# The last 28 static columns of each expert: 1188 instead of 1216 in an attention and mixture-of-experts kernel

## The chip, the core and the metric

The kernel runs on one core of a Trainium2 chip. The metric is the device time of one execution in microseconds (us), the median of several runs. Engines are named as the profile names them: PE is TensorE's matmul, PEld its weight load, DVE is VectorE, ACT is ScalarE, POOL is GpSimd, SP is SyncE, which here only issues DMAs.

## The reference

Attention over 8 batches, 8 heads, 576 rows and 64 columns is followed by a mixture of 8 experts over the 4608 rows that attention gives. Each row goes to the two experts with the largest noisy logits:

```python
noisy_logits = x @ w_gate + np.log1p(np.exp(x @ w_noise)) * noise
top2 = np.argpartition(-noisy_logits, 2, axis=1)[:, :2]
for e in range(E):
    for k in range(2):
        mask = top2[:, k] == e
        h = np.maximum(x[mask] @ w1[e], 0.0)             # 512 -> 1024
        out[mask] += top2_w[mask, k, None] * (h @ w2[e])  # 1024 -> 512
```

How many rows an expert gets depends on the data. All inputs are drawn by `setup_inputs` from seed 0.

## The kernel before, in words

**Attention** (the first 600 us or so) runs in steps of a pair of heads, with loads, splits, scores and stores placed by hand at slots of a schedule. As each batch ends, its rows are routed: for each row and choice a slot number `e * slots + rank` is worked out, and the pair (row number, gate weight) is written with an indirect DMA into a table in DRAM, `slot_table` (L614). An expert owns `slots` consecutive entries of it. The first `cap = 32 * NBLK` of them (L30: NBLK is 38, so 1216) are the static part, which the unrolled program always computes. Entries that no row fills point at spare rows with a gate of zero; the initial contents are written early by SP (`table_part`, L466 to L471). Rows beyond `cap` go to `overflow` (L1084), a loop behind the static program that takes 128 rows in each pass and makes as many passes as the counts ask for.

**Experts.** The static part of an expert is cut into 38 blocks of 32 entries, in three groups of 12, 12 and 14 blocks (L31), that is 384, 384 and 448 columns. In float32r each operand is split into a high and a low part, and a product is three matmuls. For each group:

- `gather` (L846, POOL) fetches up to 128 rows of x with an indirect DMA, `bounce` (L856, SP) stores them to a staging buffer in DRAM, `load` (L866, SP) reads them back with four DMAs in another order, and `turnx` (L878 to L881, DVE and ACT) transposes and splits them.
- `layer1` (L883) makes 8 pieces f of the hidden layer; each is 12 matmuls over all columns of the group, `n = 32 * GROUPS[g]` (L885, L896).
- `layer2` (L902) makes the output. In its usual form a unit holds up to 128 rows as the weights of 24 matmuls with 512 moving columns (L917). For the last 10 blocks of the third group `layer2t` (L952) swaps the operands: four chains c of 24 matmuls whose moving operand has `n = 32 * WIDE[g]` = 320 columns (L956, L966). The last expert has no wide part: its third group is computed by four usual units, the last of them with 64 rows.
- The result is multiplied by the gate (L919, or L971 and L976) and added to `out` by an indirect DMA (L938, POOL).

`run` (L1018) writes these steps out in a fixed order for the 8 experts; while the matmuls of one group run, the next groups are fetched and the weights of the next stage loaded and split. Two PSUM tiles named `sp` of two banks each take the layer2 results.

**Tokens.** `tokens` (L808) copies an expert's table entries into the tile `ti` with four DMAs on SP, one for each quarter of the partitions, and `index` (L819) derives from it on DVE the row numbers for the gathers (`sx`, `ix`) and the gates (`gw`). For the experts from 2 on this is one part of 38 blocks, loaded one expert ahead. Experts 0 and 1 have two parts (`parts_of`, L112): the first 24 (12) blocks hold rows of the first six batches and are read while attention still runs; the rest, 14 (26) blocks, can be read only when the last batch is routed. These eight DMAs, for both experts in a row, are issued at one place (`tokb`, L55), and both `index` calls stand together behind them (`ixb`). This is the handover from attention to the experts: group 2 of expert 0 cannot be gathered before.

**The start.** The constructor of `Experts` (L705) runs before `attention` records anything, so what it puts on POOL stands ahead of `make_identity` (L137), whose result the first ten matmuls (L141) read.

Of the kernel before, what the change touches and what calls it, by code (L numbers as in the profile page):

```python
# [26 lines left out]
SPARE = 384  # L27
NB = 5

NBLK = 38  # L30
GROUPS = (12, 12, 14)  # L31

WIDE = (0, 0, 10)

STAGED = 20

EARLY = (GROUPS[0] + GROUPS[1], GROUPS[0])
WARM = 10

SCHED = dict(  # L40
# [19 lines left out]
@with_exitstack  # L60
def tile_attention_moe(ctx: ExitStack, tc, q, k, v, tau, wgn, noise, noise_r, w1, w2, out, x_dram, table, stage):
    nc = tc.nc
    const = ctx.enter_context(tc.tile_pool(name="const", bufs=1))
    cap = 32 * NBLK
    nover = -(-max(N - cap, 0) // 128)
    slots = cap + 128 * nover
    state = dict(cap=cap, nover=nover, slots=slots)
    with tc.manual_schedule(), ExitStack() as c:
        work = c.enter_context(tc.tile_pool(name="work", bufs=1))
        psum = c.enter_context(tc.tile_pool(name="psum", bufs=1, space=PSUM))  # L70
        experts = Experts(tc, const, work, psum, state, w1, w2, out, x_dram, table, stage)
        attention(tc, const, work, psum, state, q, k, v, tau, wgn, noise, noise_r, out, x_dram, table, experts)
        experts.run(lambda: overflow_count(tc, const, work, state) if nover else None)
    if nover:
        with ExitStack() as c:
            overflow(c, tc, const, state, w1, w2, out, x_dram, table)


def wide(e, g):

    return 0 if e == E - 1 else WIDE[g]


def units(e, g):
# [27 lines left out]
def parts_of(e):  # L112


    n = EARLY[e] if e < len(EARLY) else 0
    return [(0, n), (n, NBLK - n)] if n else [(0, NBLK)]


def attention(tc, const, work, psum, state, q, k, v, tau, wgn, noise, noise_r, out, x_dram, table, experts):
    nc = tc.nc  # L120
    rot = Rotor()
    slots, cap, nover = state["slots"], state["cap"], state["nover"]
# [317 lines left out]
    base = state["base"] = const.tile([128, E], F32, name="base")  # L440
# [3 lines left out]
    def init_parts():  # L444
        def load_noise():
            nc.sync.dma_start(nz[:, :, 0:4, :], noise)
            nc.sync.dma_start(nz[0:64, :, 4, :], noise_r)
        yield load_noise


        nb = 4 * -(-NBLK // 4)
        tin = work.tile([32, nb, 2], I32, name="tin", tag="y1")
        vec.memset(tin, 0)
        for a in range(0, nb, 12):
            m = min(12, nb - a)
            gp.iota(tin[:, a:a + m, 0], pattern=[[32, m]], base=0, channel_multiplier=1)
        tin = tin.rearrange("p a c -> p (a c)")
        if nover:
            tin2 = work.tile([nover, 128, 2], I32, name="tin2", tag="y0")
            vec.memset(tin2, 0)  # L460
            gp.iota(tin2[:, :, 0], pattern=[[1, 128]], base=0, channel_multiplier=0)
            tin2 = tin2.rearrange("p a c -> p (a c)")
        z = work.tile([128, DM], F32, name="zeros", tag="zeros")
        vec.memset(z, 0.0)

        def table_part(e):  # L466
            to = table[e * slots:(e + 1) * slots, :].rearrange("s c -> (s c)")
            for k0, nb in parts_of(e):
                nc.sync.dma_start(to[64 * k0:64 * (k0 + nb)].rearrange("(p c) -> p c", p=32), tin[:, 0:2 * nb])
            if nover:  # L470
                nc.sync.dma_start(to[2 * cap:2 * slots].rearrange("(p c) -> p c", p=nover), tin2)  # L471
        for e in range(E):
            yield lambda e=e: table_part(e)
        yield lambda: nc.sync.dma_start(x_dram[0:SPARE, :].rearrange("(a p) d -> p a d", p=128),
                                        z[:, None, :].to_broadcast([128, SPARE // 128, DM]))
        nt = (N + SPARE) // 128

        def out_part(a):
            m = min(2, nt - a)
            nc.sync.dma_start(out[128 * a:128 * (a + m), :].rearrange("(a p) d -> p a d", p=128),  # L480
                              z[:, None, :].to_broadcast([128, m, DM]))
        for a in range(0, nt, 2):
            yield lambda a=a: out_part(a)
# [157 lines left out]
    for n in range(NP):  # L641
        g = 9 * n
# [29 lines left out]
        if n % HP == HP - 1:  # L672
# [10 lines left out]
            for i in range(2 * NB):  # L683
                to = g + x + 11 + i
                if experts and b >= B - 2:
                    to = G + START["put" if late else "put0"][i]
# [15 lines left out]
class Experts:  # L702


    def __init__(self, tc, const, work, psum, state, w1, w2, out, x_dram, table, stage):  # L705
# [10 lines left out]
        for j in range(4):  # L716
# [2 lines left out]
        self.toks = [tuple(const.tile([128] + sh, t, name=f"{n}{i}") for n, sh, t in  # L719
                           (("ti", [NBLK, 2], I32), ("ix4", [NBLK], I32), ("sx", [nm], I32), ("gw", [nm], F32)))  # L720
                     for i in range(3)]
        self.chunks = [(e, l, f) for e in range(E) for l in range(2) for f in range(8)]
        self.at = {c: i for i, c in enumerate(self.chunks)}
        CW = 32 * max(GROUPS)
# [83 lines left out]
    def tokens(self, e, part):  # L808
        if e >= E:
            return  # L810
        nc = self.nc
        ti, ix, sx, gw = self.tok[e] = self.toks[e % 3]
        k0, nb = parts_of(e)[part]
        src = bass.AP(tensor=self.table.tensor, offset=self.table.offset + (e * self.slots + 32 * k0) * 2,
                      ap=[[2 * nb, 32], [1, 2 * nb]])
        for j in range(4):
            nc.sync.dma_start(ti[32 * j:32 * j + 32, k0:k0 + nb].rearrange("p k c -> p (k c)"), src)

    def index(self, e, part):  # L819
        if e >= E:  # L820
            return
        vec = self.nc.vector
        ti, ix, sx, gw = self.tok[e]
        k0, nb = parts_of(e)[part]
        vec.tensor_scalar(ix[:, k0:k0 + nb], ti[:, k0:k0 + nb, 0], 4.0, self.jq, op0=ALU.mult, op1=ALU.add)
        for j in range(4):
            k = slice(k0 + j, k0 + nb, 4)
            n = len(range(k.start, k.stop, 4))
            p = slice(32 * j, 32 * j + 32)
            vec.tensor_copy(sx[p, k0 // 4:k0 // 4 + n], ti[p, k, 0])  # L830
            vec.tensor_copy(gw[p, k0 // 4:k0 // 4 + n], ti.bitcast(F32)[p, k, 1])
# [50 lines left out]

    def layer1(self, e, g, f):  # L883
        nc = self.nc
        n = 32 * GROUPS[g]  # L885
        if f == 0:
            self.ht[e, g] = (self.next("h", 2), [])
        xh, xl = self.xt[e, g] if f < 7 else self.xt.pop((e, g))
        p, parts = self.ht[e, g]
# [12 lines left out]
    def layer2(self, e, g, i):  # L902
        nc = self.nc
        t = (GROUPS[g] - wide(e, g)) // 4
        if wide(e, g) and i >= t:
            return self.layer2t(e, g, i - t)
        _, parts = self.ht[e, g]
        _, _, sx, gw = self.tok[e]
        m = 32 * min(4, GROUPS[g] - 4 * i)
        t = self.first[g] // 4 + i  # L910
        ps = self.bank(False)
        c = slice(128 * i, 128 * i + m)
        for f in range(8):
# [4 lines left out]
        y = self.place()  # L918
        nc.vector.tensor_scalar(y[0:m].rearrange("p (j c a) -> p c j a", j=4, c=4),  # L919
                                ps[0:m].rearrange("p (c j a) -> p c j a", c=4, j=4), gw[0:m, t:t + 1], None, op0=ALU.mult)  # L920
        self.late.append((self.turn["y"], lambda: self.scatter(
            e, range(4 * t, 4 * t + m // 32), self.out, sx[0:m, t:t + 1], y[0:m])))

    def place(self):

# [8 lines left out]
    def scatter(self, e, blocks, out, idx, y):  # L934
# [3 lines left out]
        st = self.nc.gpsimd.indirect_dma_start(out=out, out_offset=bass.IndirectOffsetOnAxis(ap=idx, axis=0),  # L938
                                               in_=y, in_offset=None, compute_op=ALU.add)

        own = {(k - k0) % 12 for k in blocks for k0, nb in parts_of(e) if k0 <= k < k0 + nb}
        key = tuple(sorted(own))
        self.tc.declare_no_dep(st.ins, group=f"out{e}.{key}", reason="other rows")
        for r in SETS:
# [7 lines left out]
    def layer2t(self, e, g, i):  # L952


        nc = self.nc
        nb, n = WIDE[g], 32 * WIDE[g]  # L956
        k0 = GROUPS[g] - nb
        _, parts = self.ht[e, g]
        ti, ix, _, _ = self.tok[e]
# [233 lines left out]
```

## Time and profile before

| | |
|---|---|
| runs | 1488.08, 1491.34, 1493.65 us, median 1491.34 us |
| profiled execution | 1489.61 us, of which the span from the first to the last instruction is 1487.9 us |
| busy, share of that span | PE 98%, PEld 81%, DVE 60%, ACT 47%, POOL 44% |
| mean granted TensorE clock | 0.990 of full speed |
| DMA | 220.55 MB, 148 GB/s over the span |

The profile is of one execution. A busy PE is one that has a matmul in flight; matmuls are pipelined, so the time that a matmul adds is read from the distance between the starts of successive ones, not from the length of one. A line number is that of the kernel before; in the changed kernel the same lines stand 12 to 25 lines further down (layer1's matmul is L921, layer2t's L991, layer2's L942).

### The profile page before, as it was taken

Reading aid. Unit: us, or ns where it says so; the run is one execution under the profiler, and the core shown is the slowest. Engines: PE = TensorE matmul, PEld = TensorE weight load, DVE = VectorE, ACT = ScalarE, POOL = GpSimd, SP = SyncE. Lnnn points to the kernel's source line nnn. Section 1 sums busy time; section 2 is a strip of 40 time slices with the busy share of each in tenths; the row PEclk is TensorE's granted clock in tenths of the full one; section 3 lists DMA queues with packets and bytes.
Section 4 is the critical chain, followed back from the end, with each engine's and each line's share of the span. In section 5 each row is a group of like instructions: output and inputs, shape, how many; then the busy total and the mean of one; then the engine's idle time right before and its main releaser. Section 6 shows DMA issues by size and latency. Waiting matters only on the chain. (4 is left out here: it accounts for less than half of the span.)

```text
span 1487.9 us, 26126 instructions
## 1 busy us (share of the span) xinstructions
PE 1455.3 (98%) x8750; PEld 1198.1 (81%) x8750; DVE 888.4 (60%) x2477; ACT 703.4 (47%) x1447; POOL 656.0 (44%) x1025
## 2 busy tenths in 40 slices
PE   9999999999999998998999999999999999999995
PEld 6777767666666765787998998989989989989884
DVE  8888888888888888554444444454443543543411
ACT  7888888888888887422222122222231221221210
POOL 3347565656565766553162252342432522521512
PEclk9999999999999999999999999999999999999998
DMA  7768677777776676356475376375375564663422
GB/s 201 186 189 198 192 188 194 187 196 184 193 188 176 155 193 186 83 122 153 128 162 143 84 175 152 83 184 143 93 175 137 115 165 109 139 163 85 68 29 33
DMA packets 189207, 220.55 MB, mean 148 GB/s; under 512 B 64120, under 2 KB 112208, under 8 KB 188048
## 3 DMA queue, kind: packets, MB, share of 16 engines
q1 hardware_dynamic: 161856, 178.92, 44.0%
q0 software_dynamic: 27216, 39.94, 16.1%
q8 instruction: 71, 1.16, 0.3%
q14 instruction: 64, 0.52, 0.1%
HBM read 103.25 MB, written 60.67 MB: 110 GB/s over the span
## 5 line engine op out<-in xcount | busy, mean ns | idle before, releaser
L272 ACT ACTIVATE e<-ns,nm 128x576 f32<-128x576 f32 x288 | 223.1, 775 | 36.8 <-DVE ns L270 33.4
L295 DVE SCALAR_TENSOR_TENSOR p<-ns,thr,e 128x576 f32<-128x576 f32 x256 | 221.8, 866 | 22.1 <-ACT thr L280 21.3
L270 DVE TENSOR_SCALAR_CACHE_REDUCE ns<-sp 128x576 f32<-128x576 f32 x288 | 214.2, 744 | 20.6 <-PE sp L259 18.1
L307 PEld LDWEIGHTS tp<-ident,p 128*128 128x128 f32 x1024 | 110.6, 144 | 100.2 <-ACT ot L379 23.1
L310 ACT ACTIVATE pt<-tp 128x512 f32<-128x512 f32 x256 | 150.8, 589 | 55.5 <-PE tp L307 54.8
L373 PE MATMUL tp<-pt,vt 128*64 128x256 f32 (+1 forms) x1024 | 177.0, 430 | 0.0
L307 PE MATMUL tp<-ident,p 128*128 128x128 f32 x1024 | 168.1, 287 | 0.0
L259 PE MATMUL sp<-ks,qh 128*128 128x288 f32 x496 | 159.8, 335 | 4.4 <-DVE ns L270 4.4
L938 POOL DMA_INDIRECT out<-m_y,ix x54 | 86.8, 1607 | 160.0 <-DVE m_y L976 147.1
L938 POOL DMA_INDIRECT out<-m_y,sx x43 | 68.2, 1586 | 201.0 <-DVE m_y L919 172.7
L259 PE MATMUL sp<-ks,ql 128*128 128x288 f32 x496 | 138.5, 296 | 0.0
L898 ACT ACTIVATE m_p<-m_tp 128x384 fp32r<-128x384 f32 (+1 forms) x66 | 33.0, 500 | 216.4 <-PE m_tp L896 216.3
L919 DVE TENSOR_SCALAR m_y<-m_sp,gw 128x512 f32<-128x512 f32 (+1 forms) x43 | 32.3, 750 | 155.5 <-PE m_sp L917 145.8
L187 POOL TENSOR_TENSOR lok<-kr,hik 128x640 fp32r<-128x640 f32 x31 | 56.9, 1835 | 139.5 <-ACT hik L186 127.8
L846 POOL DMA_INDIRECT m_p<-x_rows,sx x71 | 69.8, 983 | 80.1 <-DMA stage<-m_p 56.5
L259 PEld LDWEIGHTS sp<-ks,qh 128*128 128x128 f32 x496 | 93.8, 189 | 6.1 <-DVE ns L270 5.0
L898 ACT ACTIVATE m_qh<-m_tp 128x384 fp32r<-128x384 f32 (+1 forms) x11 | 5.7, 515 | 190.0 <-PE m_tp L896 190.0
L259 PEld LDWEIGHTS sp<-ks,ql 128*128 128x128 f32 x496 | 94.3, 190 | 0.1
L614 POOL DMA_INDIRECT slot_table<-pay,sl x80 | 86.4, 1080 | 17.6 <-issue 10.8
L373 PEld LDWEIGHTS tp<-pt,vt 128*64 128x64 f32 x1024 | 57.1, 136 | 42.9 <-issue 25.9
L896 PE MATMUL m_tp<-m_pt,m_pt 128*128 128x384 f32 (+1 forms) x396 | 73.5, 343 | 0.0
L896 PE MATMUL m_tp<-m_vt,m_pt 128*128 128x384 f32 (+1 forms) x264 | 73.1, 351 | 0.0
(384 smaller groups left out, 3526.6 us busy)
## 6 DMA issues: line engine op xcount, KB each, us to landing
m_qr<-w SPq DMA_DIRECT2D x85, 256.0 KB
qh<-hiq SPq DMA_DIRECT2D x124, 144.0 KB
ql<-loq SPq DMA_DIRECT2D x124, 144.0 KB
stage<-m_p SPq DMA_DIRECT2D x63, 256.0 KB
m_kr<-w SPq DMA_DIRECT2D x43, 256.0 KB
kr<-k SPq DMA_DIRECT2D x32, 320.0 KB
out<-zeros SPq DMA_DIRECT2D x19, 512.0 KB
qr<-q SPq DMA_DIRECT2D x32, 288.0 KB
```

The costliest lines, as they stand in the source:

```text
L187: nc.gpsimd.tensor_tensor(lo, x, hi.bitcast(F32), op=ALU.subtract)
L259: nc.tensor.matmul(o, q_, k_, start=(i == 0), stop=(i == len(parts) - 1))
L270: nc.vector.tensor_scalar(ns, sp[:, :, 0:HALF], -1.0 / math.sqrt(D), None, op0=ALU.mult, op1=ALU.min, accum_out=nm)
L272: nc.scalar.activation(e, ns, AF.Exp, bias=nm, scale=-1.0)
L295: nc.vector.scalar_tensor_tensor(p, ns, thr, e, op0=ALU.is_le, op1=ALU.mult, accum_out=ssum[n][:, c:c + 1])
L307: nc.tensor.transpose(tp[:, kt, :], p[:, 128 * kt:128 * kt + 128], ident)
L310: nc.scalar.activation(pt[n][:, s, :, c0:c0 + 128], tp, AF.Copy)
L373: nc.tensor.matmul(o[64 * s:64 * s + 64, 0:c1 - c0], w, x, start=(kt == 0), stop=(kt == 4))
L614: st = nc.gpsimd.indirect_dma_start(out=table, out_offset=bass.IndirectOffsetOnAxis(ap=d["sl"][0:m, i, c:c + 1], axis=0), in_=d["pay"][0:m ...
L846: self.nc.gpsimd.indirect_dma_start(out=r[0:m], out_offset=None, in_=x, in_offset=bass.IndirectOffsetOnAxis(ap=self.tok[e][2][0:m, t:t + 1 ...
L896: nc.tensor.matmul(ps[:, 0:n], w[:, 128 * c:128 * c + 128], x[:, c, 0:n], start=(i == 0), stop=(i == len(ops) - 1))
L938: st = self.nc.gpsimd.indirect_dma_start(out=out, out_offset=bass.IndirectOffsetOnAxis(ap=idx, axis=0), in_=y, in_offset=None, compute_op= ...
```

## The change

The static part becomes 1188 entries: 37 blocks of 32 and a last block of 4. NBLK stays 38 (it is derived now), and so do the groups, the gathers and the scatters. What depends on columns gets narrower: layer1 of the third group from 448 to 420 columns, layer2t from 320 to 292, the last expert's last usual unit from 64 to 36 rows. `slots` goes from 4672 to 4644, with the overflow part at 27 times 128 entries as before.

The short block is not a whole row of the table's arrangement, so it is handled apart: its initial contents are one small DMA more for each expert at the start; `tokens` issues four more small DMAs (4 entries each) for each expert, behind the four of the part that ends at block 37; and the unused 28 entries of the last block are given once, in the constructor, by a memset and four iotas on POOL for each of the three `ti` tiles.

```diff
-NBLK = 38
+CAP = 1188
+NBLK = -(-CAP // 32)
+TAIL = CAP - 32 * (NBLK - 1)
...
+def columns(g):
+    return 32 * GROUPS[g] - (32 - TAIL if g == len(GROUPS) - 1 else 0)
...
-    n = EARLY[e] if e < len(EARLY) else 0
-    return [(0, n), (n, NBLK - n)] if n else [(0, NBLK)]
+    n, m = EARLY[e] if e < len(EARLY) else 0, NBLK - 1
+    return [(0, n), (n, m - n)] if n else [(0, m)]
...
+            nc.sync.dma_start(to[2 * (cap - TAIL):2 * cap].rearrange("(p c) -> p c", p=TAIL),
+                              tin[0:TAIL, 2 * SHORT:2 * SHORT + 2])
...
+        for ti, *_ in self.toks:
+            self.nc.gpsimd.memset(ti[:, NBLK - 1, :], 0)
+            for j in range(4):
+                self.nc.gpsimd.iota(ti[32 * j:32 * j + 32, NBLK - 1, 0:1], pattern=[[0, 1]], base=32 * SHORT,
+                                    channel_multiplier=1)
...
+        if k0 + nb == NBLK - 1:
+            a = e * self.slots + CAP - TAIL
+            for j in range(4):
+                nc.sync.dma_start(ti[32 * j:32 * j + TAIL, NBLK - 1, :], self.table[a:a + TAIL, :])
...
-        n = 32 * GROUPS[g]
+        n = columns(g)
...
-        m = 32 * min(4, GROUPS[g] - 4 * i)
+        m = min(128, columns(g) - 128 * i)
...
-        nb, n = WIDE[g], 32 * WIDE[g]
+        nb, n = WIDE[g], columns(g) - 32 * (GROUPS[g] - WIDE[g])
```

Three places where the program's order matters. POOL at the start, before; `ident` is what the first matmuls read:

```order
L1188 UNCONDITIONAL_BRANCH
masks.py:197 MEMSET ident 128x128
masks.py:199 ISA
masks.py:199 AFFINE_SELECT ident<-ident 128x128
L426 IOTA iota_127 128x8
```

and now:

```order
L1213 UNCONDITIONAL_BRANCH
L738 MEMSET ti_72 128x2
L740 ISA
L740 IOTA ti_72 32x1 x4
L738 MEMSET ti_76 128x2
L740 IOTA ti_76 32x1 x4
L738 MEMSET ti_80 128x2
L740 IOTA ti_80 32x1 x4
masks.py:197 MEMSET ident 128x128
masks.py:199 AFFINE_SELECT ident<-ident 128x128
```

Fifteen instructions moved in ahead of the two that make `ident`.

SP at the handover, before; `ti_72` and `ti_76` are the token tiles of experts 0 and 1, `m_qr` and `m_kr` raw weights, `stage` the bounce and `m_zeros` the loads behind it:

```order
L794 DMA m_qr_8329<-w 128x512
L817 DMA ti_72<-slot_table 32x28 x4
L817 DMA ti_76<-slot_table 32x52 x4
L794 DMA m_qr_8661<-w 128x512
L794 DMA m_kr_8327<-w 128x512
L856 DMA stage<-m_p 128x512 x3
L866 DMA m_zeros<-stage 32x4x128 x4
```

and now:

```order
L814 DMA m_qr_8352<-w 128x512
L837 DMA ti_72<-slot_table 32x26 x4
L841 DMA ti_72<-slot_table 4x2 x4
L837 DMA ti_76<-slot_table 32x50 x4
L841 DMA ti_76<-slot_table 4x2 x4
L814 DMA m_qr_8684<-w 128x512
L814 DMA m_kr_8350<-w 128x512
L881 DMA stage<-m_p 128x512 x3
L891 DMA m_zeros<-stage 32x4x128 x4
```

Sixteen token DMAs stand there in place of eight, expert 0's whole set ahead of expert 1's.

DVE at the handover, now; the order is that of before. `ix_73` belongs to expert 0, `ix_77` to expert 1, `m_sp` are the two PSUM tiles of layer2:

```order
L944 TENSOR_SCALAR m_y_9590<-m_sp_9016,gw_75 128x4x4x32
L850 TENSOR_SCALAR ix_73<-ti_72,jq 128x14
...
L850 TENSOR_SCALAR ix_77<-ti_76,jq 128x26
...
L944 TENSOR_SCALAR m_y_8063<-m_sp_9051,gw_75 128x4x4x32
L903 STREAM_TRANSPOSE m_hiq_8686<-m_xg_8382 128x128 x4
L906 TENSOR_TENSOR m_pt_9091<-m_hiq_8686,m_pt_9091 128x4x128
L944 TENSOR_SCALAR m_y_8116<-m_sp_9016,gw_75 128x4x4x32
```

Both index steps, and so the arrival of all sixteen DMAs, stand ahead of the eviction of `m_sp_9051`.

## Rows read from the trace of the kernel before

**Rows 1.** The page, busy time of each engine and its share of the span.
```profile
PE 1455.3 (98%) x8750; PEld 1198.1 (81%) x8750; DVE 888.4 (60%) x2477; ACT 703.4 (47%) x1447; POOL 656.0 (44%) x1025
```

**Rows 2.** Stretches: length, then busy PE, PEld, DVE, ACT, POOL; clock, DMA, GB/s.
```profile
680.00:690.00 10.00, 7.90 (x24) 6.25 (x25) 4.46 (x13) 1.68 (x3) 3.21 (x4) 0.66 0.47 67
...
900.00:1000.00 100.00, 100.00 (x525) 91.69 (x524) 42.69 (x111) 22.36 (x45) 37.41 (x39) 1.00 0.57 132
```

**Rows 3.** PE timeline, where layers begin: start, length, line, operands, count.
```profile
690.19 0.37 PE L896 MATMUL m_tp<-m_vt,m_xr 128*128 128x448 f32 x1
...
709.69 2.25 PE L896 MATMUL m_tp<-m_pt,m_xr 128*128 128x384 f32 x12
...
715.94 2.27 PE L896 MATMUL m_tp<-m_pt,m_ks 128*128 128x384 f32 x12
...
832.33 0.60 PE L966 MATMUL m_sp<-m_p,m_pt 128*128 128x320 f32 x3
...
846.39 0.84 PE L917 MATMUL m_sp<-m_pt,m_p 128*128 128x512 f32 x3
```

**Rows 4.** PE timeline, attention: five matmuls of 288 columns, and what follows.
```profile
19.59 0.30 PE L259 MATMUL sp<-lok,qd 128*128 128x288 f32 x1
...
20.25 0.60 PE L307 MATMUL tp<-ident,p 128*128 128x128 f32 x4
```

**Rows 5.** PE timeline, last expert's unit of 64 rows.
```profile
1450.58 0.84 PE L917 MATMUL m_sp<-m_pt,m_qh 128*64 128x512 f32 x3
```

**Rows 6.** POOL timeline at the start.
```profile
0.80 0.20 POOL masks.py:197 MEMSET ident<- 128x128 f32 x1 [0.29 <-POOLq L1178]
1.08 0.29 POOL masks.py:199 TENSOR_SCALAR_AFFINE_SELECT ident<-ident 128x128 f32<-128x128 f32 x1
...
7.38 0.39 POOL L456 IOTA tin<- 32x12 int32 x4
```

**Rows 7.** Timeline at the start, PE and DVE; in brackets the idle time before.
```profile
1.43 4.07 PE L141 MATMUL tp<-ident 128*128 128x128 f32 x20 [1.43 <-POOL ident masks.py:199]
...
5.96 2.35 PE L248 MATMUL sp<-kr,qr 64*64 64x288 f32 x12 [0.47 <-ACT qr L174]
...
7.43 0.48 DVE L464 MEMSET zeros<- 128x512 f32 x1
```

**Rows 8.** SP timeline behind the first table parts.
```profile
39.32 0.43 SPq L180 DMA_DIRECT2D vt<-v  x1
40.95 1.80 SPq L208 DMA_DIRECT2D ks<-hik  x2
```

**Rows 9.** SP timeline at the handover.
```profile
657.30 3.61 SPq L817 DMA_DIRECT2D ti<-slot_table  x8
...
671.15 2.48 SPq L866 DMA_DIRECT2D m_zeros<-stage  x4
```

**Rows 10.** DVE timeline at the handover.
```profile
661.93 0.23 DVE L825 TENSOR_SCALAR ix<-ti,jq 128x14 int32<-128x14 int32 x1 [6.15 <-DMA ti<-slot_table]
...
664.23 0.75 DVE L919 TENSOR_SCALAR m_y<-m_sp,gw 128x512 f32<-128x512 f32 x1
...
676.04 0.89 DVE L878 STREAM_TRANSPOSE m_loq<-m_zeros 128x128 f32<-128x128 f32 x4 [8.21 <-DMA m_zeros<-stage]
...
681.30 0.74 DVE L919 TENSOR_SCALAR m_kr<-m_sp,gw 128x512 f32<-128x512 f32 x1
```

**Rows 11.** PE timeline at the handover, layer2 units 4 and 6 of expert 0.
```profile
665.53 0.85 PE L917 MATMUL m_sp<-m_pt,m_p 128*128 128x512 f32 x3
...
682.10 1.65 PE L917 MATMUL m_sp<-m_pt,m_p 128*128 128x512 f32 x3 [5.35 <-DVE m_kr L919]
```

**Rows 12.** SP and DVE timelines, tokens and index of a later expert.
```profile
807.34 1.78 SPq L817 DMA_DIRECT2D ti<-slot_table  x4
...
833.59 0.23 DVE L825 TENSOR_SCALAR ix<-ti,jq 128x38 int32<-128x38 int32 x1
```

**Rows 13.** The page, costliest groups: line, operands, count, busy, mean ns, idle before.
```profile
L846 POOL DMA_INDIRECT m_p<-x_rows,sx x71 | 69.8, 983 | 80.1 <-DMA stage<-m_p 56.5
```

More of the change, by code (lines that the diff above doesn't have):

```diff
@@ L37 @@
 EARLY = (GROUPS[0] + GROUPS[1], GROUPS[0])
+SHORT = 1
+assert all((NBLK - 1 - n) % 12 == SHORT for n in (*EARLY, 0))
 WARM = 10
@@ L63, in tile_attention_moe @@
     const = ctx.enter_context(tc.tile_pool(name="const", bufs=1))
-    cap = 32 * NBLK
+    cap = CAP
     nover = -(-max(N - cap, 0) // 128)
@@ L824, in index @@
         k0, nb = parts_of(e)[part]
+        nb += k0 + nb == NBLK - 1
         vec.tensor_scalar(ix[:, k0:k0 + nb], ti[:, k0:k0 + nb, 0], 4.0, self.jq, op0=ALU.mult, op1=ALU.add)
@@ L921, in layer2 @@
         self.late.append((self.turn["y"], lambda: self.scatter(
-            e, range(4 * t, 4 * t + m // 32), self.out, sx[0:m, t:t + 1], y[0:m])))
+            e, range(4 * t, 4 * t - (-m // 32)), self.out, sx[0:m, t:t + 1], y[0:m])))
     def place(self):
@@ L939, in scatter @@
                                                in_=y, in_offset=None, compute_op=ALU.add)
-        own = {(k - k0) % 12 for k in blocks for k0, nb in parts_of(e) if k0 <= k < k0 + nb}
+        own = {(k - max(k0 for k0, _ in parts_of(e) if k0 <= k)) % 12 for k in blocks}
         key = tuple(sorted(own))
@@ L1181 @@
            for n, a in arrays.items()}
-    cap = 32 * NBLK
+    cap = CAP
     slots = cap + 128 * -(-max(N - cap, 0) // 128)
```

## The prediction

> **What bounds the kernel now.** I read the busy line of the page first, then the busy time by stretch, then PE's timeline. PE has a matmul in flight for 98% of the span [rows 1]. By stretch the reader is to see that in the expert stage this is not an average: in a stretch of 100 us PE is busy for all of it at a granted clock of 1.00 (2.4 GHz), with DVE at 43%, POOL at 37% and the DMA engines at 57% [rows 2]. From 690.19 us on, where group 2 of expert 0 begins [rows 3], PE's timeline shows no row with an idle time. In this stage the time is the sum of the distances between matmul starts, and a matmul made shorter is time won, so long as nothing else falls behind.
>
> The other places to read are the handover and the start. At the handover PE stands still once for 5.35 us [rows 11]: unit 6 of expert 0's layer2 waits until DVE has evicted unit 4 from the same PSUM tile, and that eviction stands behind transposes which wait 8.21 us for rows to come back from the staging buffer [rows 10]. Before that DVE waits 6.15 us for the token DMAs [rows 10], which SP issues at 657.30 [rows 9]. So this stretch is bound by a chain: token DMAs, index, gather, bounce, load, transposes, eviction.
>
> **The change part by part.** *Layer1 of the third group, 448 to 420 columns.* With 448 columns the 96 matmuls of a group take 709.69 - 690.19 = 19.50 us. With 384, three pieces of 12 take 715.94 - 709.69 = 6.25 us, so eight take 16.67 us [rows 3]. A column is worth (19.50 - 16.67) / 64 = 0.0442 us for 96 matmuls, 28 columns 1.24 us, and eight experts 9.9 us.
>
> *Layer2t, 320 to 292 columns.* Its 96 matmuls take 846.39 - 832.33 = 14.06 us [rows 3]. From 320 to 384 columns 96 matmuls grow by 16.67 - 14.06 = 2.61 us, 0.0408 us for a column; 28 columns give 1.14 us, and seven experts (the last has no wide part) 8.0 us. Whether the slope goes on below 320 is shown by attention, where five matmuls of 288 columns, each with weights of its own, take 20.25 - 19.59 = 0.66 us [rows 4]: 96 would take 12.7 us, 0.043 us less for each column. So no floor is met between 320 and 288, and 292 lies there.
>
> Together 17.9 us off PE. The smallest slope over all fifteen stretches gives 0.0408 x 28 x 15 = 17.1, the largest 0.0442 x 28 x 15 = 18.6; these are the ends.
>
> These rows speak against one rule. The Trainium skill, "TensorE: Matmul & The Clock Gate", section "Back-to-back issue gap", gives for sustained streams of weight load and matmul about 81 ns a matmul at 128 columns and 131 ns at 512. By that a column is worth 0.13 ns, 28 columns on 1440 matmuls 5.2 us, and the whole sum would come to -3.2. The trace does not agree: 448 columns take 19.50 us / 96 = 203 ns and 320 take 146 ns [rows 3].
>
> *The last expert's unit with 36 in place of 64 rows.* The rows are weights there, and the moving operand stays at 512 columns. Three matmuls with 64 rows take 0.84 us [rows 5], three with 128 take 0.85 us [rows 11]: nothing. Narrower ACT and DVE steps lie beside PE: nothing.
>
> *POOL at the start.* Three memsets and twelve iotas stand ahead of the two instructions that make `ident`, which is ready at 1.37 us [rows 6]. Four iotas take 0.39 us [rows 6], about 0.09 us for each further one, so twelve take 1.0; a memset with a dependent instruction behind it costs at most the 0.28 us between the two `ident` instructions [rows 6], say 0.2 for a tiny one, so three take 0.6. `ident` comes 1.6 us later. PE's warm-up ends at 5.50 and its next matmul starts at 5.96, waiting for ACT [rows 7]: 0.46 is absorbed and 1.1 is left. DVE runs memsets until 7.91 anyway [rows 7], which covers another tenth or two of what the first scores lose. I take +1.0, between 0 (all covered) and 1.9 (iotas at 0.13 each, if the shorter fourth of the four counts for nothing, and 0.28 a memset, 2.4 in all, less 0.46).
>
> *SP at the start.* One small DMA more for each expert, at most four in one place, at some 0.35 us. Behind the first table parts, where three are added, SP stands idle from 39.75 to 40.95 before the next step [rows 8], 1.2 us against 1.05. I take 0, and up to 0.5.
>
> *SP at the handover.* Eight DMAs take 3.61 us, 0.45 each [rows 9]. Expert 0's index needs eight in place of four, so it starts 1.8 us later, at about 663.7, and its gathers, bounces and loads with it: the transposes at 677.8 and the eviction of unit 4 at 683.1. Expert 1's index needs the sixteenth, issued by 664.5; from the end of the fourth issue (659.1) to the index were 2.8 us [rows 9, 10], so it starts at 667.3. Behind it stands the eviction of unit 2, now at 664.23 [rows 10] and then at about 668.5. Unit 4 uses that PSUM tile and starts at 665.53 [rows 11], so a **new stall** of 3.7 us appears there. It does not add to the old one: it is taken out of it, since unit 6 waits for the eviction of unit 4 at 683.1 either way.
>
> After the stall of 5.35 us the granted clock falls (0.66 over the ten microseconds [rows 2]), and unit 6 takes from 682.10 to 690.19 [rows 11, 3], 8.1 us, where three matmuls take 1.65 us in place of 0.85 [rows 11]. With the stall split in two, unit 4 pays that (some 2.5 us, inside the remaining wait), and unit 6 waits only about 1.5 us and may keep the clock. The ends are then +1.8 - 2.5 = -0.7, and +3.2, if a token DMA takes the 0.62 us that each of the four loads at 671.15 takes [rows 9]: the eighth is then issued by 662.3 in place of 659.1 for the fourth. With the clock lost again it is +1.8. I take **+1.0**.
>
> *Tokens of the other experts.* Four more DMAs, 1.8 us on SP. For a later expert the tokens are issued at 807.34 and the index runs at 833.59 [rows 12]; nothing waits. 0.
>
> **Sum:** -17.9 + 1.0 + 0 + 1.0 = -15.9 us. Against the profiled execution, 1489.6 becomes 1473.7. The median of the runs lies 1.7 above it, so the median forecast is 1491.3 - 15.9 = **1475.4 us**. The ends are -18.6 + 0 - 0.7 = -19.3 (1472.0) and -17.1 + 1.9 + 0.5 + 3.2 = -11.5 (1479.8).
>
> **The rivals.** *The loop behind runs.* If one expert has over 1188 rows, `overflow` makes a pass. A pass issues 19 indirect DMAs for tokens, rows and weights, one after another on POOL, at 0.98 us each [rows 13], 18.7 us at the least. The landing comes on top, some 2.8 us from an issue to its use as for the token DMAs [rows 9, 10]: all of it for tokens, rows and first weights, which depend on each other, and a part for each later pair of weights, which share two buffers. Three times 2.8 gives 27 us as the least, nineteen times 2.8 gives 72 as the most; with the weights half hidden I put it at 45 us as an estimate. The time would be 1475.4 + 45 = **1520**, slower than before. It decides at one row more than 1188. Against it: routing the reference's inputs by the reference's formula gives 1139, 1145, 1185, 1157, 1186, 1170, 1110 and 1124 rows, and the closest gap between a second and a third logit is 2e-5, so that a rounding hardly moves a row. Two spare entries are left. 2%.
>
> *The columns are worth less below 320.* The weight loads, which are busy for 92 of 100 us [rows 2], could set a floor for a matmul of 292 columns. Then layer2t gives nothing: -9.9 + 2.0 = -7.9, **1483.4**. The 288-column row [rows 4] speaks against it, though its operands are others. 4%. The flatter rule of the Trainium skill named above is the same case carried further (1488), and the trace gives it under 1%.
>
> *The columns come back as waiting.* If gathers, DVE's transposes and splits or the weight loads paced the expert stage, PE would wait instead, and the two costs would remain: **1493**. Against it: the 384-column groups run with the same fetches and splits at 16.7 us a layer [rows 3], faster than the 18.3 that is asked of a 420-column one, and PE waits for nothing there. 3%.
>
> *The handover costs more*, for instance since gathers and bounces interleave worse: +5 in place of +1, **1479.5**. 6%.
>
> **How the numbers follow.** The forecast has 85%. A measurement of this kernel can tell about 0.5% from no change, 7.5 us, so faster means below 1483.9. Faster are the forecast, the costlier handover and two of the four per cent of the second rival, 93%; same are the rest of it, its flatter form and the third rival, 5%; slower is the loop, 2%. The range takes the forecast's own ends and some 2 us for the spread of the runs (1488.08 to 1493.65): 1470.5 to 1481.5.
>
> **What would show it.** Layer1 of the third group should take 18.3 us in place of 19.50, and layer2t 12.9 in place of 14.06; PE should have no idle row after the handover. At the handover I expect the token DMAs over 7.2 us, expert 0's index 1.8 us later, a stall of PE of 3 to 4 us ahead of unit 4 and a shorter one ahead of unit 6. At the start the first matmul should begin near 3 us. The loop's lines must not appear in the chain of waits. The prediction is wrong if PE idles after 690 us, if layer2t stays above 13.4 us, or if the handover ends more than 3 us later against the start.

## The result, and the profile after

| | before | after |
|---|---|---|
| median of the runs | 1492.49 us (1488.08 to 1499.32, 4 runs) | 1473.46 us (1472.27 to 1476.8, 4 runs) |
| profiled execution: span | 1487.9 us | 1470.5 us |
| start of the first pair's row step on DVE | 10.55 | 12.77 |
| last put into the table, POOL | 655.26 | 652.49 |
| first token DMA of expert 0's second part, SP | 657.30 | 658.45 |
| group 2 of expert 0 begins on PE | 690.19 | 689.92 |
| from there to the end of the span | 797.7 | 780.6 |

The two medians are 19.0 us apart. The ratio estimated from all these runs is 0.9884, with an interval of 0.9859 to 0.9909: 17.3 us of 1492.49 are gone, between 13.6 and 21. A second measurement, told below, gives 0.9905 (0.9882 to 0.9929), which is 14.2 us. The forecast of -15.9 us is a ratio of 0.9893, inside both.

The last two lines of the table say where the time went. From group 2 on, 17.1 us are gone; everything ahead of it came out level, and the middle lines show that it did so by several changes that cancelled: the first pair starts 2.2 us later, the last put comes 2.8 us earlier, and the token DMAs come 3.9 us later behind that put. The page's line of busy time [rows 1] has 19.6 us less on PE, most of it behind the handover:

```profile
PE 1435.7 (98%) x8750; PEld 1187.0 (81%) x8750; DVE 886.9 (60%) x2477; ACT 702.3 (48%) x1447; POOL 661.1 (45%) x1040
```

PE's timeline after, the places that answer to [rows 3] (start, length, line, operands, count):

```profile
689.92 0.35 PE L921 MATMUL m_tp<-m_vt,m_xr 128*128 128x420 f32 x1
...
708.23 2.24 PE L921 MATMUL m_tp<-m_pt,m_xr 128*128 128x384 f32 x12
...
724.93 0.56 PE L991 MATMUL m_sp<-m_qh,m_pt 128*128 128x292 f32 x3
...
737.73 0.86 PE L942 MATMUL m_sp<-m_pt,m_qh 128*128 128x512 f32 x3
...
776.70 2.47 PE L921 MATMUL m_tp<-m_pt,m_xr 128*128 128x420 f32 x12
...
795.24 0.86 PE L942 MATMUL m_sp<-m_pt,m_qh 128*128 128x512 f32 x3
```

Layer1 with 420 columns takes 708.23 - 689.92 = 18.31 us for expert 0 and 795.24 - 776.70 = 18.54 for expert 1, against 19.50 with 448. Layer2t with 292 columns takes 737.73 - 724.93 = 12.80 against 14.00 and 14.06 with 320. No row of PE behind 689.92 has an idle time, and no line of the loop behind the static part has work on PE.

The handover. First the last put of the kernel before, which belongs to the SP row at 657.30 [rows 9]:

```profile
655.26 0.90 POOL L614 DMA_INDIRECT slot_table<-pay,sl  x1 [0.22 <-issue]
```

Then, after the change and in the order of the chain: the last put on POOL, SP's token DMAs, DVE's index and evictions, PE's units 4 and 6 [rows 9 to 11]; then the stretches of 10 us (length, busy PE, PEld, DVE, ACT, POOL, granted clock, DMA, GB/s).

```profile
652.49 0.90 POOL L628 DMA_INDIRECT slot_table<-pay,sl  x1 [0.22 <-issue]
...
658.45 2.31 SPq L837 DMA_DIRECT2D ti<-slot_table  x4
660.81 1.33 SPq L841 DMA_DIRECT2D ti<-slot_table  x4
662.18 1.69 SPq L837 DMA_DIRECT2D ti<-slot_table  x4
663.92 1.34 SPq L841 DMA_DIRECT2D ti<-slot_table  x4
```

```profile
663.38 0.23 DVE L850 TENSOR_SCALAR ix<-ti,jq 128x14 int32<-128x14 int32 x1 [10.37 <-DMA ti<-slot_table]
...
666.85 0.24 DVE L850 TENSOR_SCALAR ix<-ti,jq 128x26 int32<-128x26 int32 x1 [2.37 <-DMA ti<-slot_table]
...
668.26 0.75 DVE L944 TENSOR_SCALAR m_y<-m_sp,gw 128x512 f32<-128x512 f32 x1
...
683.49 0.74 DVE L944 TENSOR_SCALAR m_kr<-m_sp,gw 128x512 f32<-128x512 f32 x1
```

```profile
669.06 1.65 PE L942 MATMUL m_sp<-m_pt,m_p 128*128 128x512 f32 x3 [6.17 <-DVE m_y L944]
...
684.29 0.96 PE L942 MATMUL m_sp<-m_pt,m_p 128*128 128x512 f32 x3 [1.40 <-DVE m_kr L944]
```

```profile
660.00:670.00 10.00, 3.83 (x15) 2.85 (x14) 3.94 (x23) 0.16 (x1) 3.64 (x4) 0.89 0.36 113
670.00:680.00 10.00, 10.00 (x36) 7.96 (x35) 2.73 (x7) 1.10 (x2) 3.49 (x4) 0.77 0.97 233
680.00:690.00 10.00, 8.60 (x38) 6.70 (x37) 5.55 (x18) 1.69 (x3) 3.21 (x4) 1.00 0.45 73
```

The reader is to see three things. The eviction of unit 2 at 668.26 stands behind the second index, as the prediction said, and PE's one stall of 5.35 us is now two, 6.17 ahead of unit 4 and 1.40 ahead of unit 6. The granted clock falls behind the first (three matmuls take 1.65 us, and the mean from 670 to 680 is 0.77) and is back at 1.00 from 680 on, so for unit 6, which takes 689.92 - 684.29 = 5.63 us in place of 8.09. And the first token DMA is issued 5.96 us after the last put, where it was 2.04 before: that is new, and the prediction has no word on it.

The start of the program, POOL and PE [rows 6, 7], then the first pair's row step on DVE, before (L295) and after (L307):

```profile
0.80 0.10 POOL L738 MEMSET ti<- 128x2 int32 x1 [0.29 <-POOLq L1203]
0.97 0.65 POOL L740 IOTA ti<- 32x1 int32 x4
...
3.41 0.20 POOL masks.py:197 MEMSET ident<- 128x128 f32 x1
```

```profile
4.04 4.64 PE L153 MATMUL tp<-ident 128*128 128x128 f32 x20 [4.04 <-POOL ident masks.py:199]
8.60 2.71 PE L260 MATMUL sp<-kr,qr 64*64 64x288 f32 x13
```

```profile
10.55 0.81 DVE L295 SCALAR_TENSOR_TENSOR pr<-ns,thr,e 128x576 f32<-128x576 f32 x1
```

```profile
12.77 0.81 DVE L307 SCALAR_TENSOR_TENSOR pr<-ns,thr,e 128x576 f32<-128x576 f32 x1
```

The fifteen small instructions take 3.41 - 0.80 = 2.6 us, not 1.6, and the first scores begin 8.60 - 5.96 = 2.64 us later, not 1.1. The 0.46 us by which PE had waited for ACT before were not absorbed: the 20 warm-up matmuls, which took 4.07 us before, take 4.64 here and run up to the first scores.

### The profile page after: what moved, and what is told of

It is laid out like the page before. It is cut to its first block, busy times and chain, and to the rows that moved or that the text cites. A ratio compares the mean times of both kernels' runs of the same rounds, so it can differ in the third digit from the quotient of the medians.

```text
span 1470.5 us, 26196 instructions
## 1 busy us (share of the span) xinstructions
PE 1435.7 (98%) x8750; PEld 1187.0 (81%) x8750; DVE 886.9 (60%) x2477; ACT 702.3 (48%) x1447; POOL 661.1 (45%) x1040
## 5 line engine op out<-in xcount | busy, mean ns | idle before, releaser
L307 DVE SCALAR_TENSOR_TENSOR p<-ns,thr,e 128x576 f32<-128x576 f32 x256 | 222.3, 869 | 21.6 <-ACT thr L292 20.8
```

The lines of the kernel that those rows point to most:

```text
L307: nc.vector.scalar_tensor_tensor(p, ns, thr, e, op0=ALU.is_le, op1=ALU.mult, accum_out=ssum[n][:, c:c + 1])
```

## The experiments

Three questions were open. Is the gain the columns alone? What does each cost really come to? And what made the tokens late? The runs come from three chips, each with runs of the kernel before beside it; ratios are against those. Each experiment has one profile.

**The columns alone (a_cols).** The kernel before, with only the widths of the third group changed. It leaves out the last 28 columns of the last block, which there hold real entries of each expert.

```diff
+def columns(g):
+    return 32 * GROUPS[g] - (28 if g == len(GROUPS) - 1 else 0)
...
-        n = 32 * GROUPS[g]
+        n = columns(g)
...
-        nb, n = WIDE[g], 32 * WIDE[g]
+        nb, n = WIDE[g], columns(g) - 32 * (GROUPS[g] - WIDE[g])
```

> The kernel before with only the matmuls narrowed (420 and 292 columns); the table, the token DMAs and the start are those of before. Theory (the two costs are real and add up, about +2 us in the changed kernel): 19 us below the kernel before, ratio 0.987, some 2 us faster than the changed kernel. Rival (attention and the handover absorb them): 17 us below, ratio 0.9885, the same as the changed kernel. By either its layer1 of the third group takes 18.3 to 18.5 us and layer2t 12.8 us, and the first score tile is on DVE near 7.9 us in place of 10.0.

Measured: ratio 0.9903 (0.9878 to 0.9928), span 1473.4 us; group 2 begins at 692.76 and the stage takes 780.6 us from there, the same as in the changed kernel. Layer1 of expert 0 is 711.06 - 692.76 = 18.30 us:

```profile
692.76 0.35 PE L900 MATMUL m_tp<-m_vt,m_xr 128*128 128x420 f32 x1
...
711.06 2.24 PE L900 MATMUL m_tp<-m_pt,m_xr 128*128 128x384 f32 x12
```

So the gain behind the handover is the columns and nothing else; e_wide below shows the same from the other side. Of the two expectations for the ratio, 0.987 with the costs saved and 0.9885 with nothing to save, the interval holds the second alone. But group 2 begins 2.6 us later here than in the profile of the kernel before (692.76 against 690.19) with nothing ahead of it changed, so that attention varies by as much as the costs are worth, and this ratio does not settle them.

**The costs without the columns (b_over, then e_wide).** The first try was the changed kernel with 1216 entries, so that its tail is a whole block of 32.

```diff
-CAP = 1188
+CAP = 1216
```

> The changed kernel with 1216 entries and a last block of 32: all the added DMAs and POOL instructions, no column saved. Theory: 2 us slower than the kernel before, ratio 1.0013. Rival (absorbed): ratio 1.000. By either the first matmul starts near 4 us, the first pair of heads is 2.2 us late, and 16 token DMAs stand at the handover.

Measured: ratio 1.0054 (1.0032 to 1.0076), some 8 us slower, far more than the sum of the costs. One pair of heads took 24.47 us, where the same pair takes 18.25 in the kernel before. SP shows why: the table DMAs of the tails, 32 pieces of 8 bytes each, hold SP up.

```profile
39.53 0.42 SPq L482 DMA_DIRECT2D slot_table<-tin  x1
...
40.73 3.45 SPq L482 DMA_DIRECT2D slot_table<-tin  x1
44.22 1.08 SPq L485 DMA_DIRECT2D slot_table<-tin  x1
45.34 0.36 SPq L174 DMA_DIRECT2D qr<-q  x1
```

The same two lines take 0.32 and 0.29 us in the changed kernel, whose pieces are four, and its load of the next queries goes out at 41.27 in place of 45.34:

```profile
40.58 0.32 SPq L482 DMA_DIRECT2D slot_table<-tin  x1
40.94 0.29 SPq L485 DMA_DIRECT2D slot_table<-tin  x1
41.27 0.36 SPq L174 DMA_DIRECT2D qr<-q  x1
```

That this is the cause was tried by writing the same 256 bytes as one piece (i_tbl):

```diff
-            nc.sync.dma_start(to[2 * (cap - TAIL):2 * cap].rearrange("(p c) -> p c", p=TAIL),
-                              tin[0:TAIL, 2 * SHORT:2 * SHORT + 2])
+            nc.sync.dma_start(to[2 * (cap - TAIL):2 * cap].rearrange("(p c) -> p c", p=1),
+                              tin2[0:1, 64 * SHORT:64 * SHORT + 2 * TAIL])
```

> The kernel with 1216 entries and a tail of 32 (ratio 1.0054), whose eight table DMAs for the tails now move the same 256 bytes as one piece in place of 32 pieces of 8 bytes. Theory (the 32 pieces filled SP's queue: one issue took 3.45 us, the loads of pair 3 came 4 us later and a pair took 24.5 us): that pair's interval returns to 18 to 19 us, the first group 2 starts at 689 to 691, the ratio is 0.999 to 1.002. Rival (the loss comes from elsewhere, such as the longer token loads at the handover): the interval stays over 21 us or the ratio stays at 1.004 to 1.006.

Measured: the issue takes 0.27 us, the pair 19.86 us, and the ratio is 1.0026 (1.0013 to 1.0039):

```profile
40.86 0.27 SPq L482 DMA_DIRECT2D slot_table<-tin  x1
```

Of the 6.2 us that the pair had lost, 4.6 are back, so the pieces are what held SP up. The pair's time lies between the theory's 18 to 19 and the rival's 21; e_wide, with four pieces, has 20.12 there. The ratio is above the theory's 1.002. By the two ratios about half of the whole loss is gone, but their intervals overlap, so that this share is not settled. For the changed kernel itself, b_over was the wrong probe, since its tail is eight times as long. The right one keeps the tail of 4 and only computes the old widths (e_wide):

```diff
-    return 32 * GROUPS[g] - (32 - TAIL if g == len(GROUPS) - 1 else 0)
+    return 32 * GROUPS[g]
```

> The changed kernel with all its costs (tail entries, table DMAs of four pieces, four more token DMAs for an expert, late ident) but with 448 and 320 columns as before: the third group's matmuls run over 28 more columns of the last block, whose rows are spare ones. Theory (the gain is the columns alone, and the costs cancel): the expert stage takes 797.4 us from group 2 of expert 0 on, as with the old widths; group 2 starts at 690 +- 3; the span is 1487 to 1490, ratio 0.9985 to 1.0015. The prediction's own terms, +1.0 for POOL and +1.0 for SP, would give 1.0013. Rival (the kernel with 1216 entries and a tail of 32 showed what the costs are): ratio 1.0054. On the table: from the last put to the first token DMA 5.5 to 6 us if the table's new stride of 1188 entries is what made the puts land late in the changed kernel, 2.0 to 2.6 us if the narrow columns did.

Measured: ratio 1.0018 (1.0006 to 1.0030), that is +2.7 us, between 0.9 and 4.5; the stage behind the handover, from 695.52 to the end of the span at 1492.8, takes 797.3 us, as in the kernel before:

```profile
695.52 0.36 PE L921 MATMUL m_tp<-m_vt,m_xr 128*128 128x448 f32 x1
```

The costs do not cancel, as the theory had it; they are near the prediction's +2.0. The tokens came 5.25 us after the last put, so the narrow columns are not what makes them late.

**The start on POOL (c_late, o_start).** c_late is the changed kernel with the fifteen instructions moved behind `ident`; o_start is the kernel before with them ahead of it.

```diff
+        experts.fill()
...
-        for ti, *_ in self.toks:
-            self.nc.gpsimd.memset(ti[:, NBLK - 1, :], 0)
...
+    def fill(self):
+        for ti, *_ in self.toks:
+            self.nc.gpsimd.memset(ti[:, NBLK - 1, :], 0)
...
```

> The changed kernel with the three memsets and twelve iotas moved behind those that make the first matmuls' operand. Theory: the 2.2 us at the start come back at the end, at least 1 of them: 18.3 to 19.5 us below the kernel before, ratio 0.9875. Rival (attention absorbs the late start): as the changed kernel, 17.3 us below, ratio 0.9884. By either the first matmul starts near 1.4 us again.

> The kernel before with the three memsets and twelve iotas ahead of ident on POOL, and nothing else of the change. The prediction's term: +1.0 us, 0 to 1.9, ratio 1.0007. By the first pair's start in the changed kernel (12.77 against 10.55) it would be +2.2, ratio 1.0015. Rival (attention's own variation takes it up, as the changed kernel with these instructions moved behind ident showed no difference): the first pair at 12.2 to 12.9, but the ratio within 0.0005 of 1.

Measured: c_late 0.9889 (0.9864 to 0.9914), with the first pair's row step back at 10.56; o_start 1.0016 (0.9998 to 1.0034), with that step at 12.96. That the instructions ahead of `ident` delay the first pair is shown in both directions; over all eight profiles of kernels that have them there its row step begins between 12.18 and 13.29, over the six others between 10.55 and 10.63, so the delay is 1.6 to 2.7 us. What is left of it at the end is not settled: o_start says +2.4 with zero just inside its interval, c_late shows no difference, in an interval of 3.7 us either way.

**The loop behind (d_loop).** The changed kernel with 1184 entries, two less than the fullest expert needs, so that the loop runs twice.

```diff
-CAP = 1188
+CAP = 1184
...
-GROUPS = (12, 12, 14)
+GROUPS = (12, 12, 13)
...
-WIDE = (0, 0, 10)
+WIDE = (0, 0, 9)
...
-SHORT = 1
+SHORT = 0
```

> 1184 entries in 37 whole blocks (groups of 12, 12 and 13; 416 and 288 columns): two experts have 1185 and 1186 rows, so the loop behind makes two passes. Static part by the slopes: 2 to 3 us less than in the changed kernel. Theory: 45 us for a pass, so 1492 - 20 + 90 = 1562 us; ends 27 and 72 for a pass, 1526 and 1616 us. Rival (the loop costs little): under 1500 us.

Measured: 1559.81 us in one run, against 1562 expected. PE's timeline gives the length of a pass from one pass's transposes to the next one's, 1524.19 - 1478.42 = 45.8 us; the prediction put it at 45:

```profile
1478.42 1.09 PE L1153 MATMUL px<-ident,xp 128*128 128x128 f32 x4 [17.92 <-DVE xp L1151]
...
1524.19 1.09 PE L1153 MATMUL px<-ident,xp 128*128 128x128 f32 x4 [21.94 <-DMA wb<-w,wrowi]
```

**What makes the tokens late (j_pad, l_stride, q_small).** With 1188 in place of 1216 entries the distance in the table from one expert's part to the next shrinks from 4672 to 4644 entries. j_pad is the changed kernel with the old distance, by 28 unused entries; l_stride is the kernel before with 36 unused entries, whose distance in bytes has the same remainder by 512 as that of the changed kernel; q_small is the kernel before with exactly the changed kernel's distance. In j_pad and l_stride the fill of the room behind keeps its length.

```diff
 j_pad
-    slots = cap + 128 * nover
+    slots = cap + 28 + 128 * nover
...
 l_stride
-    slots = cap + 128 * nover
+    slots = cap + 36 + 128 * nover
...
 q_small
-    slots = cap + 128 * nover
+    slots = cap + 128 * nover - 28
...
-                nc.sync.dma_start(to[2 * cap:2 * slots].rearrange("(p c) -> p c", p=nover), tin2)
+                nc.sync.dma_start(to[2 * cap:2 * cap + 252 * nover].rearrange("(p c) -> p c", p=nover), tin2[:, 0:252])
```

> The changed kernel with the table's stride for an expert put back to that of the kernel before by 28 unused entries (the entries' bytes are then a multiple of 512 again); nothing else changes. Theory (with a stride of 1188 or 1184 the scattered 8-byte puts land later: the median landing was 5 to 6 us against 3.7, and the token DMAs came 5.5 to 6.0 us after the last put against 2.0 to 2.6): the token DMAs are issued 2.0 to 2.6 us after the last put, the handover ends some 3.5 us earlier against the last put, and the span is 1466 to 1469, ratio 0.9855 to 0.9875. Rival (the late landing comes from other traffic or from chance): 5.5 to 6 us again, ratio 0.9884.

> The kernel before with 36 unused entries for an expert, so that its stride has the same remainder by 512 bytes as that of the changed kernel. Theory (the stride decides when the puts land): 5.5 to 6 us from the last put to the first token DMA in place of 2.0, median landing near 5 us in place of 3.7, group 2 of expert 0 some 3.5 us later, ratio 1.001 to 1.003. Rival (not the stride): 2.0 to 2.6 us, ratio 1.000.

> The kernel before with 28 entries less for an expert in the room behind the static ones, so that the table has the stride and size of the changed kernel's (4644 entries); the fill of that room is cut to 126 entries a piece. Theory (the stride or the size of the table as such makes the puts land late): 5.3 to 6 us from the last put to the first token DMA in place of 2.0, median landing of the puts 4.3 to 4.8 in place of 2.9, handover some 2.5 us longer from the last put, ratio 1.001 to 1.0025. Rival (it takes something else of the change, such as the tail's own pieces or where an expert's static part begins): 2.0 to 2.6 us, median landing about 3, ratio 0.999 to 1.001.

Measured, first q_small: its last put and its token DMAs, 7.31 us apart where the kernel before has 2.04, with nothing changed but this distance and the fill of the room behind:

```profile
661.19 0.90 POOL L614 DMA_INDIRECT slot_table<-pay,sl  x1 [0.22 <-issue]
...
668.50 3.58 SPq L817 DMA_DIRECT2D ti<-slot_table  x8
```

j_pad, the other way round, has 2.02 us:

```profile
661.98 0.90 POOL L628 DMA_INDIRECT slot_table<-pay,sl  x1 [0.23 <-issue]
...
664.00 1.74 SPq L837 DMA_DIRECT2D ti<-slot_table  x4
```

All kernels of this study, by the distance between two experts' parts:

| entries | kernels | last put to tokens, us | last put to group 2, us |
|---|---|---|---|
| 4640 | d_loop | 5.5 | 37.2 |
| 4644 | after, twice; c_late, e_wide, q_small | 5.3 to 7.3 | 36.7 to 38.2 |
| 4672 | before, a_cols, b_over, i_tbl, j_pad, o_start | 2.0 to 2.6 | 33.4 to 34.9 |
| 4694 | n_best | 2.0 | 35.2 |
| 4708 | l_stride | 2.4 | 34.9 |

So the distance decides, shown in both directions, in one profile each, and no profile of the one kind reaches into the other's times. The size of the whole table goes with the distance in every one of these kernels and is not told apart from it. The theory of the remainder fell: l_stride has the changed kernel's remainder and 2.4 us. What it is about 4640 and 4644 that makes the tokens late stays open. What SP waits for is the landing of the puts: where a trace holds the last put's landing (before, b_over, l_stride), the first token DMA goes out within 0.03 us of it. Of the twenty puts of the last two batches the traces of the kernel after and of j_pad hold the landing of 14 each; this is the time from the put to its landing:

```profile
DMA to landing us min/median/max: 2.3/4.8/7.0
```

```profile
DMA to landing us min/median/max: 2.1/3.1/6.7
```

The profiles of q_small, o_start, m_after and n_best hold no landings, so that the later landing which q_small was expected to show is seen there only in the tokens.

The price at the whole time is not shown. In the profiles the handover ends 36.7 to 38.2 us behind the last put in place of 33.4 to 35.2, but none of the three ratios is where its theory had it: they are 0.9897 (0.9883 to 0.9911) for j_pad, 0.9996 (0.9983 to 1.0009) for l_stride and 1.0002 (0.9985 to 1.0019) for q_small, whose interval ends at 2.8 us.

**The changed kernel again, and a version with its costs taken away (m_after, n_best).** n_best has 1186 entries, the number of the fullest expert for these inputs; the fifteen instructions behind `ident`; and no table DMA for the tail, since the fill of the room behind begins 2 entries earlier, in pieces of 130.

```diff
-CAP = 1188
+CAP = 1186
...
-    slots = cap + 128 * nover
+    slots = cap - TAIL + 130 * nover
...
-                nc.sync.dma_start(to[2 * cap:2 * slots].rearrange("(p c) -> p c", p=nover), tin2)
+                nc.sync.dma_start(to[2 * (cap - TAIL):2 * slots].rearrange("(p c) -> p c", p=nover), tin2)
```

> The changed kernel again, beside the other three. Theory (columns -17.1 us; all costs together +2.7 as the kernel with the old widths showed, 0.9 to 4.5): ratio 0.9903, 0.989 to 0.9915. Rival (the first measurement's 0.9884 is right, so the costs are nothing or a gain): 0.988 to 0.989. The prediction's own sum, -15.9, would be 0.9893. From the last put to the first token DMA 5.3 to 6 us as in the first run of it.

> The changed kernel with 1186 entries (the fullest expert's number; a tail of 2), the tail's instructions behind ident on POOL, and the tail's table entries written by the DMA that fills the room for later ones (27 pieces of 130 entries in place of 128), so that no table DMA is added; the stride becomes 4694 entries. Theory (each cost is a thing of its own and can be taken away): the expert stage takes 17.1 x 30 / 28 = 18.3 us less than with 38 whole blocks, 779.3 to 779.6; first pair at 10.6; no wait of PE for the spread of a query half near 58 us; 2.0 to 2.6 us from the last put to the tokens; ratio 0.987 to 0.9885. Rival (the costs are elsewhere or do not add up): ratio as that of the changed kernel beside it, within 0.0015.

Measured: m_after 0.9905 (0.9882 to 0.9929), n_best 0.9884 (0.9858 to 0.9909). They lie apart as expected, and their intervals overlap, so that n_best is not shown to beat the changed kernel. The tokens of m_after come 6.35 us after the last put, a little later than expected. The steps of n_best did what they were to do: the first pair's row step at 10.63, no wait of PE near 58 us, tokens 2.04 us after the last put. One did not: the stage behind the handover takes 780.8 us, no less than with 1188 entries, where 779.3 to 779.6 were expected. PE's timeline of n_best shows a layer2t with 290 columns:

```profile
733.15 0.56 PE L993 MATMUL m_sp<-m_qh,m_pt 128*128 128x290 f32 x3
...
746.09 0.86 PE L944 MATMUL m_sp<-m_pt,m_qh 128*128 128x512 f32 x3
```

It takes 12.94 us, 0.14 more than with 292 columns; layer1 with 418 takes 18.33 and 18.23 where 420 takes 18.31 and 18.54.

## Why the prediction was right

**Layer1, -9.9: right in kind, a little too much.** Measured over the eight experts, 147.3 us against 155.9: -8.6. The step that was off is the slope, 0.0442 us a column. It was drawn between 448 and 384, across two kinds of group, and from 420 to 448 it is 0.0385; besides, eight pieces with 384 columns take 16.70 to 16.79 us, a little more than the 16.67 worked out from three. Group 2 of expert 0 meets the 18.3 us that were asked; the groups of experts 1, 3 and 5 take 18.54.

**Layer2t, -8.0: right.** Measured -8.5, since 292 columns take 12.80 to 12.84 us. The 288-column row of attention was the right row to lean on: its five matmuls gave 12.7 us for 96, and layer2t with 288 columns takes 12.74 in d_loop. The rival by which columns below 320 are worth less is refuted, as is its flatter form: 292 columns are 133 ns a matmul and 320 were 146. By an estimate from the two figures that the Trainium skill gives ("TensorE: Matmul & The Clock Gate", section "Back-to-back issue gap") less than 4 ns would lie between them; the trace does not agree. Both layers together are -17.1, the smaller of the prediction's two ends, and they are the whole change of the stage, so the last expert's unit with 36 rows gave nothing, as was said.

**No new wait behind the handover: right.** PE has no idle row from group 2 of expert 0 to the end of the static part, in any profile of the study.

**POOL at the start, +1.0: too small at the first pair.** The step "about 0.09 us for each further one" failed. An iota of one element in a row takes 0.16 us here (0.65 for four), so that `ident` came 2.6 us later and not 1.6. The step "0.46 is absorbed" failed too: the warm-up matmuls take anything from 4.07 to 4.64 us over the profiles (4.09 in l_stride and 4.62 in q_small, whose start is that of the kernel before), and in the first run of the changed kernel nothing of the slack was left. So the first pair came 2.2 us later there, outside the ends of 0 to 1.9; in e_wide, j_pad and m_after it came 1.6 to 1.8 later, inside them. The row it came from, four iotas of 12 elements in 0.39 us, is still 0.39 after; why four smaller ones take longer was not tried.

**SP at the start, 0: not always.** In m_after, e_wide, j_pad, i_tbl and d_loop PE waits 1.2 to 1.8 us for a spread query half whose DMAs stand behind the table DMAs on SP, as here in e_wide; in the first run of the changed kernel and in c_late it does not. The prediction let the added DMAs fit into SP's idle 1.2 us with a margin of 0.15. In the first run of the changed kernel that idle time is all but gone (SP goes on 0.1 us after the load of v), and still PE does not wait. Where it waits, the last of the spread's DMAs is issued by 56.7 to 59.2 us, against 53.1 before and 54.2 in that run; what holds them back further is not shown.

```profile
59.47 0.37 PE L271 MATMUL sp<-ks,ql 128*128 128x288 f32 x1 [1.40 <-DMA ql<-loq]
```

**SP at the handover, +1.0: inside its ends, by wrong steps.** That expert 0's index comes 1.8 us later behind the first token DMA was wrong: it starts 4.93 us after it, against 4.63. The prediction let 2.8 us pass from the end of the last issue to the index, as before; here 1.2 us pass from the last of the tail's four. Which of the eight landed last is not shown. The split of the stall and the clock that comes back for unit 6 were right. What the prediction did not see is the table's new distance, which moves the token DMAs themselves back by some 4 us; of that some 2.5 us are left at group 2. A part came back at unit 6: in j_pad, whose tokens are not late, PE waits 3.90 us ahead of it and needs 7.2 us from there to group 2, against 1.40 and 5.63. There the sixteen DMAs, the term that the prediction meant, cost nothing: 34.5 us from the last put to group 2, against 34.9.

**The sum.** The costs were put at +2.0; with the old widths they are +2.7 (0.9 to 4.5). The terms read off single profiles add up to more (2.2 at the first pair, 1.3 for the spread, 2.5 at the handover), and attention lies between them and the end: its last pair begins anywhere from 581.7 to 590.5 us over all profiles, in an order that does not follow the start costs (587.2 in q_small, which has none; 583.8 in the first run of the changed kernel, which has all). How much of each term reaches the end is therefore not settled. That +2.0 stands so near +2.7 is in part luck: the terms at the start were too small, and the one at the handover came from a step that the prediction did not have. The first measurement, -17.3, shows no cost at all, which no term explains: its first pair is 2.2 us late, its last pair 0.3 (583.83 against 583.49), and its last put 2.8 us early. The second, -14.2, is what -17.1 and +2.7 make.

The loop behind did not run. Its price, had it run, was right (45.8 us a pass in d_loop, against 45), with one term that the prediction did not name: 9.9 of them are POOL's wait between the scatter of one pass and the first fetch of the next.

## What to carry to other kernels

Where one engine is busy without a gap through a whole stage, the distances between its starts can be summed, and the sum came true to within 5%; take the slope of a matmul's time from widths that enclose the new one. A size that also lays out a table in memory is two changes: ask what moves in memory, not only what is issued. And when a tail of rows is split off, count the pieces of its DMAs and not the bytes: 32 pieces of 8 bytes an expert held up SP by some 4 us in one kernel here, while with four pieces each issue took 0.3 us.

## What the runs showed that was not expected

- The distance between the parts of a table into which POOL scatters 8-byte entries moved their landing: a median of 4.3 to 4.8 us with 4640 or 4644 entries (four profiles) and 2.9 to 3.4 with 4672 or 4708 (six), with the same puts. The reason is open.
- Two columns less can cost time: 290 columns took 12.94 to 13.05 us for 96 matmuls, 292 columns 12.80 to 12.84. With 288 (d_loop) it is 12.74 again.
- Layer1 with 420 columns takes 18.54 us for experts 1, 3 and 5 and 18.34 for experts 2, 4 and 6, in each profile of such a kernel that was read for it (after, m_after, a_cols, c_late); the two differ in the buffers that hold the rows. With 418 columns it is 18.23 and 18.32, the other way round.
- The start of the last attention pair varies by 9 us between profiled executions of nearly the same program, while the 780 us from group 2 of expert 0 to the end repeat within half a microsecond.
